# Three more buffers for the second load of q, in the memory of the DFT table, and a new emission order

## The chip, the cores and the metric

The kernel runs on one core of one Trainium2 chip. The time is the device time of one execution in microseconds (us). Five runs of the kernel before gave 229.76, 232.25, 232.29, 233.84 and 233.99 us, with a median of 232.29 us. The core has five engines that run side by side: TensorE (PE) for matmuls, VectorE (DVE) and ScalarE (ACT) for work on elements, GpSimd (POOL), and SyncE (SP), which in this kernel does nothing but issue DMA transfers.

## The reference, cut to what matters

All inputs are bfloat16; S is 2048 positions, D is 640 channels.

```python
g = sigmoid((q * gate_w).sum(-1))
# branch a: a shifted product and a long convolution over positions, by FFT
k_shift = sum over t in 0..3 of k shifted by (3 - t), times shift_k
kv  = k_shift * v
y   = irfft(rfft(kv padded to 2S) * rfft(ssm_k padded to 2S))[:S] + kv * ssm_D
a   = q * y
# branch b: a mixer and an MLP, both with q as the input x
h   = gelu(layernorm(x) @ w1)        # 640 x 640
hs  = (four channel groups of h, shifted by 1, -1, 2, -2 positions) @ w2
x1  = x + hs
b   = x1 + gelu(layernorm(x1) @ w3) @ w4   # 640 x 1536 and 1536 x 640
out = g * a + (1 - g) * b
```

q is needed twice: at the start as x, where it is overwritten step by step by branch b in the tile QX, and at the very end, where y is multiplied by it. That is why it is loaded a second time.

## The kernel before

Positions lie on partitions: partition p holds the 16 consecutive positions 16p to 16p+15. A "slab" s (0 to 15) is the set of 128 positions 16p+s, a 128 x 640 tile. The work is cut into named steps, each made by `pl.add` or `pl.dma` with its dependencies, buffers and function; a step is a handful of instructions on one engine.

Branch b, in chunks of four slabs: `st` and `rs` are the statistics of a layer norm and `xn` the normed slab; it is turned either by TensorE (`tr`, `te`) or by a transposing DMA (`xt`, line 537) into XNT. `W1.c.n` are the matmuls with w1 (line 574), `g1` their gelu on ScalarE; `mx` copies the odd 32-channel pieces on GpSimd. `W2.s` (line 663) makes the second product of a slab, and `add` (line 670) adds it to QX. The second norm leads to `W3.c.f` (line 749), the gelu `g2` (line 753), `W4.s.j` (line 762) and its eviction `w4e` (line 768), which adds it into QX. `xo` (lines 682 and 684) scales QX by 1 - g ahead of that. `m3*` are the steps that make a small DFT matrix on GpSimd, VectorE and ScalarE; the load of w4 (`w4`, line 733) writes over their scratch space and waits for the last of them, `m3n`.

Branch a is a convolution by a DFT in two steps. `k0` to `k3` (`ka`, `kb`, `kc`, `k1`, ...) load k. `km`, `ka` and `kv` (lines 806 to 818) form kv on VectorE, 128 x 1280 at a time; `trh` and `trhe` turn the filter ssm_k. First step: `h1` and `x1` (line 718) multiply the filter and kv by the table F1, `he` and `xe` evict the results, `hw` and `xw` write them to DRAM (GHD, GXD). `tri0` and `tri1` (line 824) make the table of the last step, I1, from F1 by a transposing DMA. Second step, in four rounds: `rh` and `rx` (line 862) load GHD and GXD in another layout into two buffers of RK, `h2`, `x2` and `pv` are matmuls (line 835), `h2e`, `x2e`, `ve` their evictions, `sw` swaps halves between partitions, `pq` (line 895) is the product of the spectra, and `vw` (line 912) writes the result VD to DRAM.

The end, per pair of slabs c: `rv` (line 919) loads 640 KB of VD into one of four buffers VX; `rq` (line 923) loads 320 KB of q into one of two buffers QR, which are the memory of the tile CJ that `km` read before. Per slab s: `iv` (line 931) is the last DFT matmul, `ye` (line 941) its eviction on ScalarE with the factor g, `y` (line 945) the product with q and `ya` (line 951) the sum into QX, both on VectorE; `st` (line 953) stores the slab.

```python
    QR = CJ.rearrange("p (b t) d -> p b t d", b=2)
    r_qr = Ring("qr", 2)
```

The order of the work is written out in the string `ORDER` (lines 85 to 176). Each word is a step, its engine (P, V, A, G, S) and the numbers of its buffers; the words are emitted in that order, so each engine runs its own steps in the order in which they stand there. The waits between engines follow from the dependencies. SyncE has one queue: a DMA that has to wait holds back all that stand behind it. The numbers for cost in `pl.add` and `pl.dma` (`iss`, `rate`, `ndesc`) were used by the planner that made the string; they make no instruction.

Of the kernel before, what the change touches and what calls it, by code (L numbers as in the profile page):

```python
# [10 lines left out]
ALU = mybir.AluOpType  # L11
# [86 lines left out]
mx1.1/G m3i4/G rs0.8/G cj3/G mx1.0/G xn0.9/V/2 xt0.2.1/S/0/2 xn0.8/V/1 st0.15/V xt0.2.0/S/0/1 h1.7.0/P/4/1 he.7.0/A/4/1 hw1/S/2
gt.1/P/2/1 z1/V/2 abs2/A abs3/A rs0.12/G sin3.0/A sin2.0/A m3i0/G h1.6.0/P/6/1 he.6.0/V/6/1 xn0.12/V/0 xt0.3.0/S/1/0 W2.5/P/0
add5/V/0 h1.7.1/P/4/1 he.7.1/A/4/1 h1.6.1/P/2/1 he.6.1/V/2/1 hw3/S/1 rs0.14/G kz/G/0 W2.3/P/6 add3/V/6 km0.0.3/V/0/0 W2.2/P/0  # L100
m3i3/G st1.3/A cj0/A xn0.15/V/2 xt0.3.3/S/1/2 add2/V/0 xn0.14/V/1 W2.4/P/2 h1.12.1/P/6/0 he.12.1/V/6/0 xt0.3.2/S/1/1 add4/V/2
st1.2/A W1.2.3/P/0/0 h1.12.0/P/4/0 g1.2.3/A/0 xn0.13/V/0 xt0.3.1/S/1/0 h1.9.0/P/6/2 W1.2.2/P/1/0 g1.2.2/A/1 he.9.0/V/6/2 cj2/G
W1.2.1/P/2/0 he.12.0/V/4/0 m3i2/G v0/S km0.0.2/V/0/0 h1.13.0/P/6/0 he.13.0/A/6/0 h1.13.1/P/4/0 g1.2.1/A/2 he.13.1/A/4/0 hw6/S/0
h1.9.1/P/0/2 he.9.1/A/0/2 W1.2.4/P/3/0 g1.2.4/A/3 W1.2.0/P/2/0 g1.2.0/A/2 gt.2/P/0/0 st1.4/A m3b/V km0.0.1/V/0/1 h1.11.1/P/6/1
h1.11.0/P/4/1 rs1.2/G xn1.2/V/2 ka0.0.2/V/0/0 xn1.3/V/1 he.11.0/V/4/1 z2/V/0 he.11.1/A/6/1 gt.3/P/1/1 z3/V/1 W1.3.4/P/2/1
h1.10.1/P/6/1 mx2.1/G mx2.0/G m3i5/G km0.0.0/V/0/0 st1.5/A ka0.0.1/V/1/0 gate0/V g1.3.4/A/2 he.10.1/A/6/1 h1.8.1/P/4/2
he.8.1/A/4/2 W1.3.0/P/3/1 g1.3.0/A/3 rs1.4/G h1.14.1/P/0/0 h1.15.1/P/6/0 gate1/A ka0.0.0/V/0/0 kv0/V/0 he.14.1/A/0/0
he.15.1/A/6/0 W1.3.2/P/2/1 g1.3.2/A/2 h1.10.0/P/4/1 W1.3.1/P/3/1 g1.3.1/A/3 h1.14.0/P/0/0 he.14.0/A/0/0 he.10.0/A/4/1
xt1.0.0/S/0/2 xn1.4/V/0 km0.1.3/V/0/0 gate2/V W1.3.3/P/2/1 g1.3.3/A/2 km0.1.2/V/0/1 xn1.5/V/2 ka0.1.2/V/1/0 mx1.2/G
km0.1.1/V/0/0 km0.1.0/V/0/1 xo3/A ka0.1.1/V/0/0 m3i1/G mx2.3/G W2.6/P/6 ka0.1.0/V/1/0 add6/V/6 xt1.0.1/S/0/1 w3/S h1.8.0/P/0/2  # L110
he.8.0/A/0/2 kv2/V/0 W2.7/P/4 add7/V/4 m3c/G m3d/V m3s/A W2.9/P/2 add9/V/2 mx3.2/G xt1.0.2/S/0/0 W2.8/P/0 xt1.0.3/S/0/2
W3.0.7/P/6/0/0 g2.0.7/A/6/0 W3.0.8/P/7/0/1 g2.0.8/A/7/1 xo5/A add8/V/0 h1.15.0/P/4/0 W3.0.3/P/0/0/2 W3.0.4/P/1/0/0
W3.0.9/P/6/0/1 g2.0.4/A/1/0 he.15.0/A/4/0 W3.0.2/P/7/0/2 W3.0.5/P/1/0/0 g2.0.5/A/1/0 g2.0.9/A/6/1 st1.6/A mx3.3/G k1/S/1
km1.0.3/V/1/0 W3.0.11/P/2/0/1 g2.0.11/A/2/1 km1.0.2/V/1/0 st1.7/A km1.0.1/V/1/1 W3.0.1/P/1/0/2 W3.0.6/P/3/0/0 g2.0.1/A/1/2
ka1.0.2/V/0/0 ka1.0.1/V/1/0 km1.0.0/V/1/0 ka1.0.0/V/0/0 v1/S kv4/V/0 km1.1.3/V/1/0 g2.0.2/A/7/2 km1.1.2/V/1/1 ka1.1.2/V/1/0
W3.0.0/P/2/0/2 st1.8/A g2.0.3/A/0/2 xo4/A km1.1.1/V/1/0 ka1.1.1/V/0/0 km1.1.0/V/1/1 ka1.1.0/V/1/0 kv6/V/0 mx2.2/G
W3.0.10/P/1/0/1 g2.0.6/A/3/0 mx3.1/G W2.11/P/4 k2/S/0 hw5/S/1 mx3.0/G W2.13/P/6 m3n/G g2.0.10/A/1/1 w4/S v2/S g2.0.0/A/2/2
W4.3.0/P/0/2/0/1 km2.0.3/V/0/0 km2.0.2/V/0/0 rs1.6/G xn1.7/V/1 xo7/A add11/V/4 w4e3.0/V/0 ka2.0.2/V/0/0 W2.10/P/2 xo2/A
km2.0.1/V/0/1 ka2.0.1/V/1/0 km2.0.0/V/0/0 add13/V/6 k3/S/1 hw4/S/2 xt1.1.1/S/1/1 xn1.6/V/0 add10/V/2 st1.9/A st1.11/A rs1.8/G
W4.2.1/P/0/2/0/1 W4.5.1/P/1/2/0/1 W4.2.0/P/4/2/0/1 xn1.9/V/2 xn1.8/V/1 mx0.3/G xt1.1.0/S/1/0 W4.5.0/P/5/2/0/1 xt1.1.3/S/1/2  # L120
xo6/A ka2.0.0/V/0/0 w4e2.0/V/4 xt1.1.2/S/1/1 kv8/V/0 w4e5.0/V/5 km2.1.3/V/0/0 st1.10/A hw7/S/0 W2.12/P/6 x1.3.1/P/2/1 add12/V/6
w4e5.1/V/1 tri0/S v3/S xe.3.1/A/2/1 tri1/S st1.13/A rs1.10/G st1.12/A rs1.12/G W4.3.1/P/4/2/0/1 W4.4.1/P/1/2/0/1 x1.1.0/P/6/2
xe.1.0/A/6/2 km2.1.2/V/0/1 km2.1.1/V/0/0 ka2.1.2/V/1/0 w4e4.1/V/1 w4e2.1/V/0 x1.3.0/P/2/1 W4.4.0/P/5/2/0/1 xe.3.0/A/2/1
W3.1.10/P/0/1/3 g2.1.10/A/0/3 x1.0.0/P/6/2 xe.0.0/A/6/2 x1.1.1/P/2/2 W3.1.2/P/1/1/0 g2.1.2/A/1/0 xe.1.1/A/2/2 x1.0.1/P/6/2
W3.1.3/P/0/1/0 xe.0.1/A/6/2 xw0/S/2 km2.1.0/V/0/1 ka2.1.1/V/0/0 ka2.1.0/V/1/0 xn1.11/V/0 xt1.2.1/S/0/0 W3.1.8/P/1/1/3
g2.1.8/A/1/3 kv10/V/0 g2.1.3/A/0/0 xn1.10/V/2 W3.1.7/P/2/1/1 g2.1.7/A/2/1 w4e4.0/V/5 km3.0.3/V/1/0 km3.0.2/V/1/0 km3.0.1/V/1/1
w4e3.1/V/4 xt1.2.0/S/0/2 ka3.0.2/V/0/0 x1.2.1/P/6/1 x1.2.0/P/4/1 xe.2.1/V/6/1 xe.2.0/A/4/1 xw1/S/1 x1.6.0/P/0/0 xe.6.0/A/0/0
W3.1.0/P/3/1/0 g2.1.0/A/3/0 ka3.0.1/V/1/0 xn1.12/V/1 x1.6.1/P/6/0 x1.7.1/P/4/0 xe.7.1/A/4/0 xe.6.1/A/6/0 W3.1.5/P/2/1/1
g2.1.5/A/2/1 km3.0.0/V/1/0 x1.8.0/P/0/2 xe.8.0/A/0/2 ka3.0.0/V/0/0 kv12/V/0 x1.7.0/P/4/0 xe.7.0/A/4/0 xt1.2.2/S/0/1 xw3/S/0
xn1.13/V/0 xt1.2.3/S/0/0 W3.1.1/P/3/1/0 x1.9.1/P/6/2 xe.9.1/A/6/2 km3.1.3/V/1/0 km3.1.2/V/1/1 x1.9.0/P/0/2 xe.9.0/A/0/2  # L130
g2.1.1/A/3/0 W3.1.4/P/2/1/1 x1.8.1/P/4/2 xe.8.1/A/4/2 xw4/S/2 x1.13.1/P/6/1 xe.13.1/A/6/1 x1.12.1/P/0/1 W3.1.6/P/3/1/1
km3.1.1/V/1/0 x1.12.0/P/4/1 xe.12.0/A/4/1 g2.1.6/A/3/1 x1.13.0/P/6/1 xe.13.0/A/6/1 xe.12.1/V/0/1 xw6/S/1 ka3.1.2/V/1/0
ka3.1.1/V/0/0 g2.1.4/A/2/1 km3.1.0/V/1/1 ka3.1.0/V/1/0 kv14/V/0 rh0/S/0 rh1/S/1 W3.1.11/P/0/1/3 g2.1.11/A/0/3 W3.1.9/P/1/1/3
x1.11.1/P/4/0 x1.10.0/P/6/0 xe.10.0/A/6/0 xe.11.1/V/4/0 xo11/V W2.14/P/2 g2.1.9/A/1/3 add14/V/2 x1.10.1/P/6/0 xe.10.1/V/6/0
x1.11.0/P/4/0 xe.11.0/A/4/0 xw5/S/0 W3.2.0/P/0/0/2 st1.14/A x1.4.0/P/2/2 xe.4.0/V/2/2 xo8/A xo10/A g2.2.0/A/0/2 x1.5.1/P/4/2
xe.5.1/V/4/2 W2.1/P/6 W2.0/P/2 add1/V/6 xo13/V x1.4.1/P/4/2 st1.1/A x1.5.0/P/0/2 xe.5.0/A/0/2 xo9/V xe.4.1/V/4/2 xw2/S/2
add0/V/2 W2.15/P/6 x1.15.1/P/4/1 xe.15.1/A/4/1 x1.14.1/P/0/1 W3.2.1/P/2/0/2 add15/V/6 st1.0/A xe.14.1/A/0/1 x1.14.0/P/6/1
xe.14.0/V/6/1 x1.15.0/P/4/1 xe.15.0/A/4/1 xw7/S/1 g2.2.1/A/2/2 W3.2.2/P/3/0/2 g2.2.2/A/3/2 rq0/S/0 h2.1.4/P/0/1/0 h2e.1.4/A/0/0
h2.1.3/P/6/1/0 h2e.1.3/V/6/0 h2.0.0/P/4/0/1 W3.2.3/P/2/0/2 h2e.0.0/A/4/1 g2.2.3/A/2/2 h2.0.3/P/0/0/1 h2.1.1/P/6/1/0
h2e.0.3/A/0/1 rs1.0/G xn1.1/V/2 xt1.3.3/S/1/2 W4.8.1/P/3/0/1/3 h2e.1.1/V/6/0 h2.1.2/P/4/1/0 st1.15/A w4e8.1/V/3 h2e.1.2/A/4/0  # L140
# [39 lines left out]
def kernel(  # L180
# [16 lines left out]
    nc = tc.nc  # L197
    P = nc.NUM_PARTITIONS
# [90 lines left out]
    pl = Plan()  # L289
# [9 lines left out]
    r_xin = Ring("xin", 2)  # L299
    r_vx = Ring("vx", 4)  # L300
    r_gy = Ring("gy", 4)
    r_qr = Ring("qr", 2)
    r_xs = Ring("xs", 3)
    r_pq = Ring("pq", 2)
    r_vst = Ring("vst", 2)
# [682 lines left out]
```

## Time and profile before

| what | us |
|---|---|
| the profiled execution's own time | 232.29 |
| its span, from the first to the last instruction | 230.4 |
| around the span | 1.9 |
| TensorE busy | 211.7 |
| VectorE busy | 189.2 |
| ScalarE busy | 165.1 |
| GpSimd busy | 60.0 |
| last W4 groups begin | 199.47 |
| last `iv` matmul ends | 224.55 |
| last VectorE step ends | 227.36 |

In 231 us the DMA engines moved 65.88 MB, a mean of 286 GB/s. A line of a stage reads: its bounds, its length, the busy time and number of instructions of PE, PEld (weight loads), DVE, ACT and POOL, the granted TensorE clock, the mean busy share of the DMA engines, and what they moved in GB/s. A line of waits reads: engine, line, tile, what it waited for, the total in us, how often, and the longest. A line of a timeline reads: start, length, engine, line, operation, tiles, number of instructions; SPq are SyncE's issues of DMAs. The engine's name with a line number such as L945 stands for the source line.

### The profile page before, as it was taken

The numbers are of one execution on the slowest core, as the hardware profiler recorded it, in microseconds if no ns is written. First come the engines' busy times: TensorE is split into PE (matmuls) and PEld (weight loads), VectorE is DVE, ScalarE is ACT, GpSimd is POOL, SyncE is SP. The second block draws the span as 40 slices with busy tenths as digits, with TensorE's granted clock in tenths as the row PEclk, the third lists the DMA queues.
The fourth block names the chain that finished last, engine by engine and source line by source line (L and its number), as shares of the span: only waits on it lengthen the run. The fifth ranks groups of instructions, "written<-read, shape, count | busy, mean of one in ns | idle before, by whom it ended". The sixth has DMA issues, their size and how long they took to land.

```text
span 230.4 us, 4443 instructions
## 1 busy us (share of the span) xinstructions
PE 211.7 (92%) x1626; PEld 123.6 (54%) x1641; DVE 189.2 (82%) x340; ACT 165.1 (72%) x252; POOL 60.0 (26%) x137
## 2 busy tenths in 40 slices
PE   6679999999989799799999999999999999999950
PEld 6557457565634576555566466433355554566630
DVE  8999979979999997999997668998649894076584
ACT  6799989899387554459887951899997884546521
POOL 2645755269997334500001220000000000000000
PEclk9999999999999999999999999999999999999996
DMA  7999979999995995979989979999999963699887
GB/s 211 373 392 294 337 157 255 185 283 335 263 417 135 385 276 81 237 193 244 320 255 378 366 236 344 355 244 350 350 334 335 346 228 133 225 403 344 298 270 268
DMA packets 53029, 65.88 MB, mean 286 GB/s; under 512 B 22544, under 2 KB 39697, under 8 KB 52624
## 3 DMA queue, kind: packets, MB, share of 16 engines
q1 hardware_dynamic: 53008, 65.61, 92.4%
q8 instruction: 12, 0.20, 0.4%
q14 instruction: 9, 0.07, 0.1%
HBM read 37.03 MB, written 18.35 MB: 240 GB/s over the span
## 4 chain that ended last, share of the span: by engine, by line
PE 57%; DVE 13%; DMA 12%; POOL 6%; ACT 6%; issue 3%; SPq 1%; DVEq 0%; POOLq 0%; ACTq 0%
PE PS L762 15%; PE PS L749 14%; PE PS L835 8%; PE PS L718 6%; PE PS L574 5%; PE PS L663 5%; DMA XNT<-XN 3%; DMA RG<-in_A_ssm_k_dram 3%; DMA RK<-GHD 3%; DVE RK L815 3%; DVE RK L811 3%; DMA CJ<-in_A_q_dram 3%; DVE QX L768 2%; DVE RK L945 2%; DVE QX L951 1%
## 5 line engine op out<-in xcount | busy, mean ns | idle before, releaser
L320 ACT CAST SX<-PS 128x640 bf16<-128x640 f32 (+1 forms) x62 | 46.4, 778 | 18.5 <-PE PS L835 10.4
L762 PE MATMUL PS<-W,RG 128*128 128x320 bf16 x384 | 56.2, 299 | 2.8 <-DVE QX L768 1.5
L749 PE MATMUL PS<-XNT,W 128*128 128x512 bf16 x229 | 54.9, 379 | 1.4 <-DVE QX L670 0.8
L762 PEld LDWEIGHTS <-RG 128*128 128x128 bf16 x384 | 36.5, 98 | 22.1 <-issue 8.4
L749 PEld LDWEIGHTS <-W 128*128 128x128 bf16 x240 | 22.6, 98 | 29.1 <-issue 5.5
L753 ACT ACTIVATE RG<-PS 128x512 bf16<-128x512 f32 x48 | 27.9, 607 | 8.5 <-PE PS L749 8.4
L768 DVE SCALAR_TENSOR_TENSOR QX<-PS,ZG,QX 128x320 bf16<-128x320 f32 x32 | 17.1, 546 | 13.7 <-PE PS L762 13.7
L895 DVE TENSOR_TENSOR SX<-SX,R 128x2048 bf16<-128x2048 bf16 x20 | 24.1, 1220 | 4.7 <-ACT SX L320 2.5
L574 PE MATMUL PS<-XNT,R 128*128 128x512 bf16 x96 | 24.0, 379 | 1.2 <-DMA R<-in_B_w_dram 1.0
L718 PE MATMUL PS<-KV,F 128*128 128x320 bf16 x128 | 23.9, 299 | 0.1
L324 DVE CAST SX<-PS 128x640 bf16<-128x640 f32 (+1 forms) x22 | 19.9, 911 | 4.4 <-PE PS L718 2.7
L663 PE MATMUL PS<-R 128*128 128x320 bf16 x160 | 23.4, 299 | 0.0
L941 ACT ACTIVATE RK<-PS,ZG 128x640 bf16<-128x640 f32 x16 | 11.8, 793 | 13.5 <-PE PS L931 10.4
L815 DVE TENSOR_TENSOR RK<-RK 128x1280 bf16<-128x1280 bf16 x24 | 20.6, 860 | 0.4
L811 DVE TENSOR_TENSOR RK<-RK,CJ 128x1280 bf16<-128x1280 bf16 x24 | 20.1, 856 | 0.0
L663 PEld LDWEIGHTS <-R 128*128 128x128 bf16 x160 | 15.7, 98 | 6.4
L320 ACT CAST KV<-PS 128x1024 bf16<-128x1024 f32 x17 | 17.0, 1017 | 2.2 <-PE PS L835 2.2
L718 PEld LDWEIGHTS <-F 128*128 128x128 bf16 x128 | 12.2, 98 | 8.8
L530 DVE TENSOR_SCALAR XN<-QX,MV,RS 128x640 bf16<-128x640 bf16 x32 | 14.5, 464 | 1.5 <-DMA XNT<-XN 1.5
L574 PEld LDWEIGHTS <-R 128*128 128x128 bf16 x100 | 9.5, 98 | 10.3 <-DMA R<-in_B_w_dram 1.2
L523 POOL TENSOR_TENSOR RS<-VE,NHALF 128x2 f32<-128x2 f32 x16 | 13.4, 838 | 1.3
L835 PEld LDWEIGHTS <-M 64*64 64x64 bf16 x320 | 7.6, 105 | 11.4 <-issue 7.0
(104 smaller groups left out, 283.4 us busy)
## 6 DMA issues: line engine op xcount, KB each, us to landing
GHD<-SX SPq DMA_DIRECT2D x8, 640.0 KB, 4.4
GXD<-SX SPq DMA_DIRECT2D x8, 640.0 KB, 4.4
RK<-GHD SPq DMA_DIRECT2D x4, 1280.0 KB, 8.7
RK<-GXD SPq DMA_DIRECT2D x4, 1280.0 KB, 6.6
R<-R SPq DMA_DIRECT2D x8, 640.0 KB, 6.5
VD<-KV SPq DMA_DIRECT2D x4, 1280.0 KB, 6.1
RK<-VD SPq DMA_DIRECT2D x8, 640.0 KB, 5.8
W<-in_B_w_dram SPq DMA_DIRECT2D x2, 1920.0 KB, 8.5
```

Source lines behind the costliest of these rows:

```text
L320: nc.scalar.copy(out=o, in_=i)
L574: nc.tensor.matmul(ps(pb), lhsT=lhsT, rhs=XNT[:, xb.idx, k, :], start=(k == 0), stop=(k == DT - 1))
L663: nc.tensor.matmul(ps(pb)[:, j, 0:DH], lhsT=gst_ap(k, s), rhs=W2[:, k, j * DH:(j + 1) * DH], start=(k == 0), stop=(k == DT - 1))
L718: nc.tensor.matmul(ps(pb)[:, j, 0:DH], lhsT=F1[:, s // 4, h, s % 4, :], rhs=src[:, s, ds], start=True, stop=not dterm)
L749: nc.tensor.matmul(ps(pb), lhsT=W3[:, k, f0 * P:(f0 + 1) * P], rhs=XNT[:, xb.idx, k, :], start=(k == 0), stop=(k == DT - 1))
L753: gns.append(pl.add("g2.%d.%d" % (c, f0), {A: act_p(512)}, lambda e, f0=f0, pb=pb, gb=gb: nc.scalar.activation(out=GTP[:, gb.idx, f0 % 4, ...
L762: nc.tensor.matmul(ps(pb)[:, 0:DH], lhsT=GTP[:, gbs[f // 4].idx, f % 4, i * P:(i + 1) * P], rhs=W4[:, f, j * DH:(j + 1) * DH], start=(f == ...
L768: nc.vector.scalar_tensor_tensor(out=x, in0=ps(pb)[:, 0:DH], scalar=OMG[:, s:s + 1], in1=x, op0=ALU.mult, op1=ALU.add)
L811: m = pl.add("km%d.%d.%d" % (c, u, j), {V: dve(2 * D, .52)}, lambda e, src=src, cj=cj, tb=tb: nc.vector.tensor_tensor(out=TMP[:, tb.idx].r ...
L815: prev = pl.add("ka%d.%d.%d" % (c, u, j), {V: dve(2 * D, .52)}, lambda e, tb=tb: nc.vector.tensor_tensor(out=acc, in0=acc, in1=TMP[:, tb.i ...
L835: nc.tensor.matmul(pt[64 * C:64 * C + 64, R, :], lhsT=M3[64 * R:64 * R + 64, m, :], rhs=rhs_fn(R, C), start=start, stop=stop)
L895: nc.vector.tensor_tensor(out=PQ[:, qb.idx], in0=XS[:, sb.idx].unsqueeze(1).to_broadcast([P, 2, 1024]), in1=HH[:, hhb.idx, u], op=ALU.mult)
```

## The change

The ring of q buffers grows from two to five. The first two remain in CJ; the other three lie in the first 3840 elements of each partition of the table F1. For that, every `rq` now depends, besides the `kv` steps, on all `x1` matmuls, which read F1, and on both `tri` transposes, which read it too. The planner's issue cost of `rh` and `rx` is set to 800 ns. The string ORDER is replaced as a whole; it has the same 942 steps, and 45 of them run on another engine than before (evictions and `xo` between VectorE and ScalarE, two `mx` copies from GpSimd to VectorE). No step is added or removed.

```diff
-    QR = CJ.rearrange("p (b t) d -> p b t d", b=2)
+    CJQ = CJ.rearrange("p (b t) d -> p b t d", b=2)
+    F1Q = F1.rearrange("p g h t d -> p (g h t d)")[:, 0:3840].rearrange("p (b t d) -> p b t d", t=2, d=D)
+
+    def qr(b):
+        return CJQ[:, b.idx] if b.idx < 2 else F1Q[:, b.idx - 2]
...
-    r_qr = Ring("qr", 2)
+    r_qr = Ring("qr", 5)
...
-        qb = Buf(r_qr, kall)
-        lq = pl.dma("rq%d" % c, lambda e, qb=qb, c=c: nc.sync.dma_start(out=QR[:, qb.idx], in_=q3[:, 2 * c:2 * c + 2, :]),
+        qb = Buf(r_qr, kall + xpe + i1n)
+        lq = pl.dma("rq%d" % c, lambda e, qb=qb, c=c: nc.sync.dma_start(out=qr(qb), in_=q3[:, 2 * c:2 * c + 2, :]),
...
-                nc.vector.tensor_tensor(out=GY[:, yb.idx], in0=GY[:, yb.idx], in1=QR[:, qb.idx, s % 2, :], op=ALU.mult)
+                nc.vector.tensor_tensor(out=GY[:, yb.idx], in0=GY[:, yb.idx], in1=qr(qb)[:, s % 2, :], op=ALU.mult)
```

The new order, taken apart by engine at the places that matter (the old one above, the new one below each time):

```text
SyncE, 50 to 90 us
old: xt1.0.0 xt1.0.1 w3 xt1.0.2 xt1.0.3 k1 v1 k2 hw5 w4 v2 k3 hw4 xt1.1.1 xt1.1.0 xt1.1.3 xt1.1.2
new: xt1.0.0 w3 xt1.0.3 xt1.0.1 xt1.0.2 k1 v2 v1 w4 k2 tri1 xt1.1.3 hw4 k3 xt1.1.1 xt1.1.2 xt1.1.0
SyncE, second DFT step
old: rh0 rh1 xw5 xw2 xw7 rq0 xt1.3.3 rx0 sw0.0 sw0.1 rx1 sw1.0 sw1.1 xt1.3.2 xt1.3.1 xt1.3.0 rh2 rq1 vw0
new: rh1 rh0 xw5 xw2 xw7 xt1.3.2 rq0 rx0 sw0.1 sw0.0 sw1.0 rx1 sw1.1 rq2 xt1.3.0 xt1.3.1 xt1.3.3 rh2 rq1 vw0
SyncE, the end
old: vw1 vw2 vw3 rv0 rv1 rv2 rv3 rv4 rq2 rq3 rv7 rv6 rq7 rq4 rv5 st7 st4 rq5 st2 st6 rq6 st5 ...
new: vw1 rq3 vw2 vw3 rq7 rv0 rv1 rv2 rv3 rv4 rv7 rq4 rv5 rv6 rq5 rq6 st7 st6 st1 ...
GpSimd
old: rs1.2 mx2.1 mx2.0 m3i5 rs1.4 mx1.2 m3i1 mx2.3 m3c mx3.2 mx3.3 mx2.2 mx3.1 mx3.0 m3n
new: rs1.2 mx1.2 rs1.4 mx2.3 mx2.2 mx2.0 m3i2 m3i5 m3c mx3.3 m3n mx3.1
TensorE, after the first W3 chunk
old: W2.11 W2.13 W4.3.0 W2.10 W4.2.1 W4.5.1 W4.2.0 W4.5.0 W2.12 x1.3.1 W4.3.1 W4.4.1 ... W3.1.10
new: W2.12 W4.5.1 W4.2.1 W2.10 W4.3.1 W4.4.1 W2.11 W4.5.0 W4.3.0 W3.1.10
TensorE, ahead of the first matmul on rh2
old: pv.1.3 W3.3.8 W3.3.10 x2.1.1 h2.2.3
new: pv.1.3 W3.3.8 W3.3.10 x2.1.4 pv.1.0 x2.1.1 W3.2.10 h2.2.0
TensorE, the end
old: W4.0.0 W4.14.0 iv0 iv1 iv3 iv2 W4.1.1 iv5 iv4 iv6 iv7 W4.1.0 iv8 iv9 W4.14.1 iv15 iv14 W4.15.0 iv12 W4.15.1 iv10 iv11 W4.0.1 iv13
new: W4.14.0 W4.0.0 W4.1.1 iv1 iv0 iv3 iv2 W4.1.0 iv4 iv5 iv7 iv6 W4.15.0 iv9 iv15 iv8 iv14 W4.14.1 iv11 iv10 iv12 iv13 W4.15.1 W4.0.1
VectorE, from the last add of the first norm to the first W4 evictions
new: add8 km1.0.3 km1.0.2 km1.0.1 ka1.0.2 ka1.0.1 km1.0.0 ka1.0.0 kv4 km1.1.3 km1.1.2 km1.1.1 ka1.1.2 xn1.9 ka1.1.1 km1.1.0 ka1.1.0 kv6 km2.0.3 km2.0.2 km2.0.1 xn1.6 xn1.8 xn1.7 ka2.0.2 ka2.0.1 w4e5.1 add10 w4e2.1 w4e3.1 add12 km2.0.0 w4e4.1 add11
```

## The prediction

> **What bounds the kernel now.** I read the page's head first, then the busy time by stage, then the waits of the stages that have any, then SyncE's own issues at the end.
>
> ```profile
> span 230.4 us, 4443 instructions
> PE 211.7 (92%) x1626; PEld 123.6 (54%) x1641; DVE 189.2 (82%) x340; ACT 165.1 (72%) x252; POOL 60.0 (26%) x137
> ```
>
> ```profile
> core 0: us, PE busy (x) PEld busy (x) DVE busy (x) ACT busy (x) POOL busy (x), PEclk, DMA share, GB/s
> 0.00:20.00 20.00, 14.40 (x155) 11.52 (x157) 18.32 (x54) 16.70 (x22) 9.02 (x37) 1.00 0.94 326
> 20.00:60.00 40.00, 39.84 (x321) 24.25 (x323) 36.59 (x86) 36.79 (x64) 24.91 (x52) 1.00 1.00 252
> 60.00:96.00 36.00, 32.30 (x197) 19.23 (x198) 33.82 (x55) 19.07 (x37) 21.35 (x38) 1.00 0.88 267
> 96.00:126.00 30.00, 29.84 (x178) 17.64 (x181) 28.52 (x47) 23.50 (x41) 1.79 (x4) 1.00 0.98 270
> 126.00:158.00 32.00, 31.70 (x271) 15.85 (x271) 25.83 (x32) 23.19 (x33) 2.93 (x8) 1.00 1.03 318
> 158.00:199.40 41.40, 41.22 (x355) 19.82 (x355) 27.36 (x28) 33.43 (x41) 0.00 (x0) 1.00 0.81 280
> 199.40:224.60 25.20, 22.41 (x160) 15.30 (x159) 16.05 (x37) 11.66 (x18) 0.00 (x0) 1.00 0.92 328
> 224.60:230.40 5.80, 0.00 (x0) 0.00 (x0) 2.69 (x6) 0.78 (x1) 0.00 (x0) 0.68 0.75 269
> ```
>
> TensorE is full at full clock from 20 to 199.4 us, except for 3.7 us between 60 and 96. The rest of what it misses is the head (5.6 us) and the end: 2.8 us idle from 199.4 to 224.6, then 5.8 us after its last matmul. A gain has to come from the end or from 60 to 96. These are the waits of the end, what SyncE issues there (L919 loads of VD, L923 loads of q, L953 stores), and the waits of 60 to 96:
>
> ```profile
> DVE RK L945 <- DMA CJ<-in_A_q_dram: 4.9, 3, 2.1
> ...
> PE PS L931 <- DMA RK<-VD: 2.2, 1, 2.2
> ```
>
> ```profile
> 206.20 1.55 SPq L923 DMA_DIRECT2D CJ<-in_A_q_dram  x2
> 207.85 0.89 SPq L919 DMA_DIRECT2D RK<-VD  x2
> 211.91 1.68 SPq L923 DMA_DIRECT2D CJ<-in_A_q_dram  x2
> 213.68 0.39 SPq L919 DMA_DIRECT2D RK<-VD  x1
> ```
>
> ```profile
> PE PS L762 <- DVE QX L768: 1.5, 2, 1.3
> ...
> PE PS L762 <- DMA W<-in_B_w_dram: 1.2, 1, 1.2
> PE PS L749 <- DVE QX L670: 0.8, 1, 0.8
> ```
>
> VectorE waits 4.9 us in three pieces for a load of q. With two buffers, each q load stands in SyncE's queue until a multiply frees a buffer, and the VD loads behind it stand too: the last (rv5) leaves at 213.68, TensorE waits 2.2 us for it, and the last q load (rq6) leaves at 220.84. The chain of waits runs through a q load from 213.24 to 219.44.
>
> **The end, part by part.** *Moved:* three q loads leave the end: rq2 goes to after sw1.1, rq3 between vw1 and vw2, rq7 before rv0. In the end remain rq4, rq5, rq6, each behind a buffer freed long before: SyncE's order is now rv0 to rv4, rv7, rq4, rv5, rv6, rq5, rq6, then the stores. What gates rv5 and rv6 is their slot's last reader, iv5 and iv6.
>
> *TensorE.* Between the start of the last W4 groups (199.47) and the end it has the same 22.4 us of work, so it can't end before 221.8; it ended at 224.55. Twelve W4 matmuls take 1.63 us, an iv (four) 0.54. The new order has three W4 groups ahead of iv1 instead of two: iv1 starts at 199.47 + 3 x 1.63 + 0.2 = 204.5. iv5 then ends near 209.4, iv6 near 210.5 (one W4 between), so rv5 leaves at about 209.5 instead of 213.7 and rq6 at about 211.5 instead of 220.8. At the 5.8 us of a VD load and 5.0 of a q load everything has landed by about 217. iv11 wants rv5 at 216: no wait.
>
> *VectorE.* Before, it ran from y0 (204.30) to ya13 (227.36): 23.1 us, with 2.16 + 12.87 + 2.69 = 17.7 busy and 5.4 idle, of which 4.9 were q. Now y0 waits for ye0, which comes second on ScalarE: 204.5 + 1.58 (first iv to first y in the trace) + 0.69 (one ye) = 206.8. From the 17.7 drop out w4e10.1, w4e1.1 (0.5 each) and xo15 (0.4), which now lie earlier: 16.3 us remain, so 223.1 if nothing is late; I add 0.6 for the pieces of waiting that weren't q, 223.7. From the last VectorE instruction to the end of the span the trace has 3.04 us (a store): 226.7.
>
> *DMA.* From 199.4 to the end 9.82 MB moved (the rates of that stretch times their times). Three q loads of 0.328 MB less is 8.84 MB; at the 366 GB/s seen from 199.4 to 204 that is 24.2 us, to 223.6. VectorE and the DMA engines are thus late together, and stores bunch: I add 0.5 us. The end comes at 227.2, 3.2 us earlier.
>
> **What the moved loads push.** One rule speaks against it: the Trainium skill, page "DMA: Bandwidth & Descriptors", section "Queues, rings and completion order", says each DMA engine takes descriptors in ring order, so a load issued early goes ahead of all that is issued after it. For rq7 the rule makes rv0 0.9 us later (0.328 MB at 366 GB/s). The rows say nothing: SyncE waits 4.6 us there for VD's last write to land while the 190 to 199 us stretch has the engines half idle, so rq7's bytes go in that hole; I take 0. rq3 falls where the share is 0.81: 0. For rq2 the rule is serious: 126 to 158 us has share 1.03 at 318 GB/s, and behind rq2 stand three transposes and rh2, whose landing (150.77, 6.7 us) released TensorE directly. By the rule rh2 lands 1.0 us later, plus 0.35 to 0.57 us for issuing it. But in the new order pv.1.0 and W3.2.10 (0.43 + 1.08) come before the first matmul on rh2, 1.5 us of cover. I take 0; uncovered it costs 1.5. Reordering rh0/rh1 and sw0/sw1 moves loads by one issue each (0.4 us): 0. The iss=800 only feeds the planner's books, no instruction.
>
> **60 to 96 us.** *Gained:* GpSimd's m3n, for which the load of the W4 weights waits, now stands behind one mx copy instead of five (63.71 to 68.65 in the trace, about 1 us each), so that load leaves SyncE some 4 us before 70.7 and the 1.2 us wait goes. The 0.8 us (add8) probably goes too, since the first W3 groups now use banks that add7 and add9 free. *Risked:* k1 now has two transposes ahead of it that wait for VectorE (xn1.3, xn1.4), before one (xn1.5); by one transpose (1.2 to 2.8 us) it leaves later than 57.76. VectorE's km1.0.3 started at 64.80 with k1 there; it could now start between 63.9 and 66. From it to w4e5.1, the first W4 eviction, stand 21 of the 128x1280 operations and four xn: 16 took 14.8 us in the trace (64.80 to 79.6), five more take 4.0, the xn 1.6: w4e5.1 at 84.8 to 86.9. TensorE, with W2.12, W4.5.1, W4.2.1, W2.10 and W4.3.1 (2 x 1.36 + 3 x 1.63 = 7.6) from 75.7, is at 83.3 when W4.4.1 needs w4e5.1's bank: it waits 1.5 to 3.6 us, where before it waited 0.8 + 1.2 + 1.5 = 3.5 in this stage. The stage stands at -2.0 to +0.6 (the upper end with 0.5 more for W3.1.10's bank). VectorE, 33.8 busy of 36, also hands ScalarE two evictions and two xo more than it takes over between 60 and 126 us, a help of some 2 us. Against it, the transposes for W3.1 wait for xn1.6 to xn1.8, now together at 83 to 85, and take 3.8 us each to land, close to W3.1.10 at 94. I take the stage at 0.
>
> The other rearrangements (head, 20 to 60, 158 to 199) exchange neighbours on engines that stay full; nothing there can gain over 0.5 us, each can lose a bubble: bounds -0.5 to +2, taken 0 as the old order's 0.7 us in these stages is the nearest row.
>
> **Sum.** Against its own execution: 230.4 - 3.2 = 227.2 of span; around it lie 232.29 - 230.4 = 1.9 us: 229.1. That execution is also the median of the five.
>
> **Rivals.** *Slower: the VectorE chain between 64 and 90.* w4e5.1 ends 20.9 us after km1.0.3 starts (20.4 and its own 0.5), and km1.0.3 can't start before k1 has landed. From k1 at 69.1 on, w4e5.1 ends after 90.0 and TensorE's wait at W4.4.1 passes 6.7 us: the old 3.5 plus the 3.2 won at the end; beyond that each us is a us of the kernel. At 71 it is 8.6 us, 1.9 too much: 234.2. For it: VectorE is busy 94% there, loads of k take 7.8 us in the median, and a transpose takes up to 4.2 us to issue when the queue is full. Against: k1 must come 5 us later than it did by one or two transposes. Chance 0.17.
>
> *The end is paced by the DMA engines.* If they keep the stretch's own mean, 9.82 MB in 31.0 us or 317 GB/s, 8.84 MB last to 227.3; the last 3 us ran at half rate (164 GB/s), so the last store is done some 1.5 us after: 228.8, and 230.7 in all. For: the share is 0.98 to 1.03 from 199.4 to 206.5. Against: 0.89 at 308 GB/s from 206.5 to 224.6, where SyncE held loads back. Chance 0.18.
>
> *Both stages gain.* The old waits go and the new bank wait is short (-2.0): 227.1. Chance 0.17.
>
> **Numbers.** My case, 229.1, has 0.48 and by itself spans 227.9 to 230.5. Two per cent is 4.6 us, about what a measurement of this kernel can tell from no change (its runs lie from 229.8 to 234.0). Faster by that (below 227.6): most of the third rival and the edge of mine, 0.2. Slower (above 236.9): the far end of the slow rival, 0.07. The range to hold 8 in 10 reaches from inside the third rival to the slow one: 226.4 to 234.4.
>
> **What would show it.** Right: no VectorE wait on q loads over 0.5 us after 199; rq6 issued by 213; VectorE without holes from y0 to the end; a span near 227. Wrong in the end: TensorE waits on VD loads, or the store queue ends more than 4 us after VectorE. Wrong in the middle: TensorE idle above 4 us between 75 and 96, released by L768. Wrong about rq2: a TensorE hole before the first h2.2 matmul. If the start of the last W4 groups is more than 1.5 us away from 199.5, the middle decided the result, not the buffers.

## The result and the profile after

The changed kernel takes 229.45 us (median of 25 runs, 228.08 to 230.74). The kernel before, on the same chip, takes 232.06 us (46 runs). The ratio is 0.9908, with a 95% interval of 0.9889 to 0.9928. Here and below a ratio is taken from the fast runs alone (some executions, of every kernel, are a few us slower) and against runs of the kernel before from the same batch, so it isn't the quotient of the two medians. The prediction was 229.1 (226.4 to 234.4). The gain is real, but smaller than the 2% that the forecast counted as faster.

The profiled execution of the changed kernel took 229.26 us. Its span is 227.3 us, against 230.4 before. Line numbers are four higher than before: the loads of VD are L923, those of q L927, the `iv` matmuls L935, the multiply by q L949, ScalarE's eviction of an `iv` L945, the sum into QX L955, W2 L667 with its add L674, W4 L766 with its eviction L772, W3 L753, the second step's matmuls L839, its loads L866 and its swaps L882. In the kernels of the experiments all of these are two lower.

The head of the page after:

```profile
span 227.3 us, 4442 instructions
PE 212.9 (94%) x1624; PEld 125.3 (55%) x1641; DVE 190.8 (84%) x343; ACT 164.2 (72%) x251; POOL 64.1 (28%) x135
```

The stages after, with the bounds of the table before except the last. The columns are length, busy time of PE, PEld, DVE, ACT and POOL, granted clock, DMA share, GB/s:

```profile
60.00:96.00 36.00, 34.03 (x205) 20.02 (x206) 35.56 (x59) 21.68 (x40) 19.38 (x28) 1.00 1.09 290
96.00:126.00 30.00, 29.79 (x180) 17.75 (x182) 25.64 (x42) 24.20 (x43) 5.62 (x11) 1.00 0.83 269
126.00:158.00 32.00, 31.89 (x283) 15.97 (x284) 27.96 (x36) 24.43 (x33) 1.72 (x5) 1.00 1.03 309
158.00:199.40 41.40, 39.52 (x340) 19.43 (x336) 27.39 (x28) 31.12 (x39) 0.00 (x0) 1.00 0.83 290
199.40:224.60 25.20, 22.14 (x160) 15.26 (x157) 17.89 (x40) 12.38 (x17) 0.00 (x0) 1.00 0.94 334
224.60:227.30 2.70, 0.00 (x0) 0.00 (x0) 0.00 (x0) 0.00 (x0) 0.00 (x0) 0.77 0.51 179
```

Two of these rows stand out, in opposite directions. TensorE gained 1.7 us of work from 60 to 96 (34.03 against 32.30) and lost 1.7 us from 158 to 199.4 (39.52 against 41.22). So the end still begins when it did: the last run of W3 matmuls starts at 191.59, before at 191.65. (The first 20 us, not shown, have 1.3 us more TensorE time as well, but the long first W3 run, which now has five matmuls more, begins only 0.5 us earlier, at 64.46 against 64.93.) The last matmul now ends at 221.84, before at 224.55; behind it the kernel needs 5.5 us, before 5.8.

What SyncE issues from 198 us on:

```profile
198.55 8.67 SPq L923 DMA_DIRECT2D RK<-VD  x6
207.68 0.35 SPq L927 DMA_DIRECT2D CJ<-in_A_q_dram  x1
209.58 1.45 SPq L923 DMA_DIRECT2D RK<-VD  x2
211.08 0.46 SPq L927 DMA_DIRECT2D F<-in_A_q_dram  x1
212.65 0.34 SPq L927 DMA_DIRECT2D CJ<-in_A_q_dram  x1
214.44 10.59 SPq L957 DMA_DIRECT2D out_dram<-QX  x16
```

The last VD loads (rv5, rv6) leave at 209.58, before at 213.68. The last q load (rq6) leaves at 212.65, before at 220.84. The waits of the same stretch, where before VectorE waited 4.9 us for q and TensorE 2.2 us for VD:

```profile
DVE QX L772 <- PE PS L766: 11.1, 2, 8.5
...
DVE RK L949 <- ACT RK L945: 1.0, 1, 1.0
```

There is no wait for q and no TensorE wait for VD left. The two waits shown are over by y0 (206.75), and from there VectorE runs without a hole to its end at 223.51.

TensorE's waits of over 0.5 us from 60 to 199 us (start, length, instructions, and in brackets the wait before them):

```profile
61.20 1.52 PE L667 MATMUL PS<-R 128*128 128x320 bf16 x10 [0.62 <-DVE QX L674]
64.46 12.03 PE L753 MATMUL PS<-XNT,W 128*128 128x512 bf16 x54 [0.60 <-DVE QX L674]
84.69 1.79 PE L766 MATMUL PS<-W,RG 128*128 128x320 bf16 x12 [0.59 <-DVE QX L772]
165.59 0.63 PE L839 MATMUL PS<-RK,M 64*64 64x512 bf16 x8 [1.21 <-DMA RK<-GHD]
184.20 1.79 PE L766 MATMUL PS<-W,RG 128*128 128x320 bf16 x12 [0.52 <-DVE QX L772]
```

The first three sum to 1.8 us; before, that stage had 3.5 us. The last two are new: 1.7 us in a stage that had none of that size.

### The profile page after: what moved, and what is told of

Read it like the earlier page. It is cut to its first block, busy times and chain, and to the rows that moved or that the text cites. A ratio compares the mean times of both kernels' runs of the same rounds, so it can differ in the third digit from the quotient of the medians.

```text
span 227.3 us, 4442 instructions
## 1 busy us (share of the span) xinstructions
PE 212.9 (94%) x1624; PEld 125.3 (55%) x1641; DVE 190.8 (84%) x343; ACT 164.2 (72%) x251; POOL 64.1 (28%) x135
## 4 chain that ended last, share of the span: by engine, by line
PE 58%; DVE 17%; DMA 15%; issue 4%; SPq 2%; ACT 2%; DVEq 0%; ACTq 0%
PE PS L753 20%; PE PS L766 16%; PE PS L839 6%; PE PS L722 5%; DMA RG<-in_A_ssm_k_dram 5%; PE PS L667 5%; DMA RK<-GHD 4%; DMA R<-R 4%; PE PS L578 4%; DVE RK L949 3%; DVE QX L955 2%; DVE RK L815 2%; DVE RK L819 2%; DVE QX L772 2%; DMA GHD<-SX 2%
## 5 line engine op out<-in xcount | busy, mean ns | idle before, releaser
L324 ACT CAST SX<-PS 128x640 bf16<-128x640 f32 (+1 forms) x64 | 47.4, 770 | 14.8 <-PE PS L722 7.0
L766 PE MATMUL PS<-W,RG 128*128 128x320 bf16 x384 | 56.2, 299 | 1.4 <-DVE QX L772 1.1
L753 PE MATMUL PS<-XNT,W 128*128 128x512 bf16 x228 | 55.5, 379 | 1.2 <-DVE QX L674 0.6
L766 PEld LDWEIGHTS <-RG 128*128 128x128 bf16 x384 | 36.6, 98 | 20.7 <-issue 6.2
L753 PEld LDWEIGHTS <-W 128*128 128x128 bf16 x240 | 22.6, 98 | 28.6 <-issue 5.3
L772 DVE SCALAR_TENSOR_TENSOR QX<-PS,ZG,QX 128x320 bf16<-128x320 f32 x32 | 17.2, 546 | 13.0 <-PE PS L766 13.0
L667 PE MATMUL PS<-R 128*128 128x320 bf16 x160 | 23.8, 299 | 0.6 <-DVE QX L674 0.6
L328 DVE CAST SX<-PS 128x640 bf16<-128x640 f32 (+1 forms) x20 | 18.4, 919 | 3.9 <-PE PS L839 1.8
L815 DVE TENSOR_TENSOR RK<-RK,CJ 128x1280 bf16<-128x1280 bf16 x24 | 20.6, 879 | 0.0
L819 DVE TENSOR_TENSOR RK<-RK 128x1280 bf16<-128x1280 bf16 x24 | 19.9, 828 | 0.4
L667 PEld LDWEIGHTS <-R 128*128 128x128 bf16 x160 | 15.7, 98 | 7.2 <-issue 0.8
L945 ACT ACTIVATE RK<-PS,ZG 128x640 bf16<-128x640 f32 x16 | 11.8, 792 | 8.5 <-DVE QX L772 5.3
L324 ACT CAST KV<-PS 128x1024 bf16<-128x1024 f32 x16 | 15.7, 1019 | 0.7 <-PE PS L839 0.7
L674 DVE SCALAR_TENSOR_TENSOR QX<-PS,QX 128x640 bf16<-128x640 f32 x16 | 12.9, 816 | 3.2 <-PE PS L667 3.2
L507 ACT ACTIVATE RG<-QX 128x640 bf16<-128x640 bf16 x16 | 11.8, 740 | 5.0 <-DVE QX L674 4.9
L578 PEld LDWEIGHTS <-R 128*128 128x128 bf16 x100 | 9.6, 98 | 10.2 <-DMA R<-in_B_w_dram 1.2
L330 DVE TENSOR_SCALAR R<-PS 128x1024 bf16<-128x1024 f32 x9 | 10.7, 1220 | 4.6 <-PE PS L839 4.6
```

Source lines behind the costliest of these rows:

```text
L324: nc.scalar.copy(out=o, in_=i)
L328: nc.vector.tensor_copy(out=o, in_=i)
L578: nc.tensor.matmul(ps(pb), lhsT=lhsT, rhs=XNT[:, xb.idx, k, :], start=(k == 0), stop=(k == DT - 1))
L667: nc.tensor.matmul(ps(pb)[:, j, 0:DH], lhsT=gst_ap(k, s), rhs=W2[:, k, j * DH:(j + 1) * DH], start=(k == 0), stop=(k == DT - 1))
L753: nc.tensor.matmul(ps(pb), lhsT=W3[:, k, f0 * P:(f0 + 1) * P], rhs=XNT[:, xb.idx, k, :], start=(k == 0), stop=(k == DT - 1))
L766: nc.tensor.matmul(ps(pb)[:, 0:DH], lhsT=GTP[:, gbs[f // 4].idx, f % 4, i * P:(i + 1) * P], rhs=W4[:, f, j * DH:(j + 1) * DH], start=(f == ...
```

## The experiments

To compare the ends of kernels that arrive there at different times, I measure from the start of the last run of W3 matmuls to the end of the span, called "the end" below. It is 38.75 us before (230.4 - 191.65) and 35.7 us after (227.3 - 191.59), so all of the 3.1 us of span is won in it. This matters because in some profiled executions the granted clock of the first 20 us is below 1.00 and everything after starts later.

### The end: buffers or order

The diff has two parts. The first try to do each alone missed its aim, and tells something else than its expectation. The number of the q buffer also stands in the words of the `y` steps, and the last word wins. I had moved only the `rq` words.

**Early loads into two buffers (e1_buffers_alone).** Old order, q loads moved early:

```diff
-... sw1.1 xt1.3.2 ... vw1 vw2 vw3 rv0 rv1 rv2 rv3 rv4 rq2/S/0 rq3/S/1 rv7 rv6 rq7/S/0 rq4/S/1 rv5 st7 st4 rq5/S/0 st2 st6 rq6/S/1
+... sw1.1 rq2/S/2 xt1.3.2 ... vw1 rq3/S/3 vw2 vw3 rq7/S/4 rv0 rv1 rv2 rv3 rv4 rv7 rv6 rq4/S/1 rv5 rq5/S/0 rq6/S/2
```

> The old emission order, with five q buffers; only the q loads are moved: rq2 to behind sw1.1, rq3 to behind vw1, rq7 to behind vw3, rq5 and rq6 to directly behind rv5. Theory A (the buffers win at the end, the new order wins nothing overall): 229.0 to 230.5 us, no wait of VectorE for q after 199 us, the last W4 groups begin within 1 us of 199.5. Theory B (the gain is the new order's, the buffers alone do nothing since the VD loads follow as before): 231.5 to 232.5 us.

In fact the kernel still used two buffers. By the order of its steps, rq2 and rq7 overwrite the buffer of rq0 before y0 reads it, so nine slabs were multiplied with rows of q that belong to others, and rq4 had to wait for a buffer. It took 234.5 us, ratio 1.0101 (1.0047 to 1.0154). It says nothing about the buffers.

**Five buffers, late loads (e2_order_alone).** New order, with the q loads back at the places they have in the old queue:

```diff
-... sw1.1 rq2 xt1.3.0 ... vw1 rq3 vw2 vw3 rq7 rv0 rv1 rv2 rv3 rv4 rv7 rq4 rv5 rv6 rq5 rq6
+... sw1.1 xt1.3.0 ... vw1 vw2 vw3 rv0 rv1 rv2 rv3 rv4 rq2 rq3 rv7 rv6 rq7 rq4 rv5 rq5 rq6
```

> The new emission order with two q buffers: rq2 and rq3 stand behind rv4, rq7 and rq4 behind rv6, rq5 and rq6 behind rv5, each waiting for its buffer as in the old kernel. Theory A: 231.3 to 232.8 us, VectorE waits 3 to 5 us for q after 199 us. Theory B: 229.2 to 230.2 us. In both, the start of the last W4 groups stays within 0.7 us of the 199.2 of the changed kernel, or comes up to 1 us earlier if the early load of rq2 cost something.

Here the `y` words kept all five buffers. So this is the changed kernel with its q loads late: 231.5 us, ratio 0.9974 (0.9935 to 1.0013), end 38.6 us. Its waits at the end:

```profile
PE PS L933 <- DMA RK<-VD: 3.0, 2, 2.4
DVE RK L947 <- DMA CJ<-in_A_q_dram: 2.7, 2, 2.4
```

Free buffers alone don't win. The two waits that the change removed are both back. They aren't all due to the q loads: this queue also has rv6 ahead of rv5, as the old one has, while the new order needs rv5 first, and rv5 left at 212.26, in the changed kernel at 209.58. And the wait has a second cost, which the granted clock shows:

```profile
219.56 3.94 PE L933 MATMUL PS<-RK,I 128*128 128x320 bf16 x16 [2.36 <-DMA RK<-VD]
```

These 16 matmuls take 2.34 us in the changed kernel. Here they take 1.6 us more, since the granted clock from 219.4 to 222.7 was 0.51. How the end splits between the q loads, rv5 and the clock was not tried.

**Buffers alone (e1b_buffers_alone).** The same places as in e1, with the buffer numbers of the `y` steps set to match:

```diff
-y5/V/0/0 y4/V/2/0 y7/V/3/1 y6/V/1/1 y15/V/3/0 y14/V/0/0 y12/V/0/1 y13/V/3/1
+y5/V/0/2 y4/V/2/2 y7/V/3/3 y6/V/1/3 y15/V/3/4 y14/V/0/4 y12/V/0/2 y13/V/3/2
```

> The old emission order on all engines, with five q buffers and the q loads early (rq2 behind sw1.1, rq3 behind vw1, rq7 ahead of rv0, rq5 and rq6 behind rv5), and now with the buffer numbers of the y steps set to match. Theory A (the buffers win at the end): VectorE's 4.9 us of waiting for q and TensorE's 2.2 us for VD are gone, rq6 is issued by 213; the old order still has VectorE's extra 1.4 us of evictions at the end and, with no cover in front of h2.2, a hole of 0.5 to 1.5 us before it: 229.5 to 231, ratio 0.99 to 0.995. Theory B (the new order wins): no more than 0.5 us, 231.5 to 232.5, ratio 0.997 or above.

It took 232.32 us (12 runs), ratio 1.0008 (0.9962 to 1.0053): no gain. Its profiled execution shows two opposite terms. The end is 36.8 us, 1.9 shorter than before. The waits there:

```profile
ACT RK L943 <- PE PS L933: 9.0, 7, 3.8
DVE RK L947 <- ACT RK L943: 3.4, 4, 2.1
```

VectorE no longer waits for q. But it waits 3.4 us, before 0.3, for ScalarE's eviction of an `iv`, and ScalarE waits for TensorE, which itself waits only 0.6 us for VD. In the old order TensorE doesn't deliver the `iv` fast enough to use the q that is there. The other term lies in the second step:

```profile
156.94 0.41 PE L837 MATMUL PS<-RK,M 64*64 64x512 bf16 x4
158.59 0.63 PE L837 MATMUL PS<-RK,M 64*64 64x512 bf16 x8 [1.23 <-DMA RK<-GHD]
```

Up to 150.7 TensorE is where it was before (150.68 against 150.70). The hole of 1.23 us is then the whole delay of the last W3 run (192.87 against 191.65). The load rh2 left at 151.85, before at 150.77, because rq2 takes 1.17 us to issue ahead of it. The sum, +1.2 - 1.9, is a profile 0.7 us shorter (229.7 against 230.4), which the interval of the ratio can't tell from nothing. The time is what theory B expected here.

**Order alone (e2b_order_alone).** New order, two buffers, the q loads as late as in the old queue, and the `y` words set to the two buffers:

```diff
-    r_qr = Ring("qr", 5)
+    r_qr = Ring("qr", 2)
...
-... vw1 rq3 vw2 vw3 rq7 rv0 rv1 rv2 rv3 rv4 rv7 rq4 rv5 rv6 rq5 rq6
+... vw1 vw2 vw3 rv0 rv1 rv2 rv3 rv4 rq2 rq3 rv7 rv6 rq7 rq4 rv5 rq5 rq6
```

> The new emission order with two q buffers and the q loads where the old kernel has them. Theory A: VectorE waits 4 to 6 us for q at the end as in the kernel before, TensorE 2 to 3 us for VD; no gain: 231.5 to 233, ratio 0.998 to 1.005. Theory B: most of the gain is here too, 229.5 to 230.5, ratio 0.99.

It took 237.54 us, ratio 1.0236 (1.0175 to 1.0296): slower than the kernel before by more than either theory had. The end is 43.1 us. Its waits there:

```profile
DVE RK L947 <- DMA CJ<-in_A_q_dram: 7.2, 4, 3.5
ACT RK L943 <- DVE QX L770: 5.3, 1, 5.3
ACT RK L943 <- DVE QX L953: 4.7, 2, 3.4
PE PS L933 <- DMA RK<-VD: 4.3, 2, 2.8
```

The new order asks for q and VD earlier than the two-buffer queue can bring them. VectorE's wait for q grows from 4.9 to 7.2 us and TensorE's for VD from 2.2 to 4.3. Two things of this kernel aren't the order's: rv6 again stands ahead of rv5, which left at 216.39, and the clock fell again. After a wait of 2.79 us for VD the next 16 `iv` matmuls took 4.00 us in place of 2.34, and the granted clock from 222.3 to 225.7 was 0.52. After the wait of 2.2 us in the kernel before it stayed at 1.00.

The ends of five kernels side by side, in us from the start of the last W3 run:

| | q loads late | q loads early |
|---|---|---|
| old order, two buffers | 38.75 (before) | - |
| old order, five buffers | - | 36.8 |
| new order, two buffers | 43.1 | - |
| new order, five buffers | 38.6 | 35.7 (after) |

Each is one profiled execution. "Order" here takes in the steps that moved to another engine. In the old order the buffers with their early loads are worth 1.9 us, in the new order 7.4. The order is worth -4.4 with two buffers and +1.1 with five. Up to 1.7 us of the 43.1 and of the 38.6 are the lower clock; without it the buffers would still be worth more in the new order (some 5.7 us) than in the old. Theory A, that the buffers win and the order is an accompaniment, and theory B, that the order wins, both fall: neither part gains anything measurable alone.

### The second DFT step

**rq2 moved (e3_rq2_late).** Is rq2, the load that the prediction worried about, the cause of the hole at 165.59?

```diff
-... rx1 sw1.1 rq2 xt1.3.0 ... vw3 rq7 rv0
+... rx1 sw1.1 xt1.3.0 ... vw3 rq7 rq2 rv0
```

> The changed kernel with rq2 moved from behind sw1.1 to behind rq7. Theory C (the 0.33 MB in the crowded stretch makes the loads of the second DFT step later; TensorE's hole of 1.2 us before h2.3 and VectorE's waits for the swaps come from it): the hole shrinks to under 0.4 us, 228.3 to 228.9 us. Theory D (the hole comes from the order of vw0 and rh3 in the queue and from the step itself, not from rq2): hole still 0.9 to 1.5 us, 229.2 to 229.8 us.

It took 229.98 us, ratio 0.9878 (0.9826 to 0.9930), not to be told from the changed kernel's 0.9908. The hole before h2.3 shrank from 1.21 to 0.42 us, but another of 1.85 us stood before matmuls on GXD at 172.58. The time fits neither theory. Its first 20 us ran at a clock of 0.91, and TensorE came to h2.3 at 165.78, in the changed kernel at 164.38, so the smaller hole doesn't say what rq2 does. The five-buffer kernel with late loads says more: it has rq2 late too, its head ran at 1.00, and TensorE came at 164.49. The hole there is 0.86 us, and rh3 landed at 165.3 (156.51 and 8.8), 0.2 us earlier than in the changed kernel.

**Three q loads moved (e6_three_q_late).**

```diff
-... xt1.3.2 rq0 rx0 ... sw1.1 rq2 xt1.3.0 xt1.3.1 xt1.3.3 rh2 rq1 vw0 ... vw1 rq3
+... xt1.3.2 rx0 ... sw1.1 xt1.3.0 xt1.3.1 xt1.3.3 rh2 vw0 ... vw1 rq0 rq2 rq1 rq3
```

> The changed kernel with rq0, rq2 and rq1 all moved to directly behind vw1, so that 0.98 MB leave the stretch from 126 to 158 us and go where the DMA engines are at 0.6 of their time. Theory C: hole before h2.3 gone, swaps land 1 to 2 us sooner, 227.4 to 228.4 us. Theory D: 229.0 to 229.8 us. Slower (above 230) would mean that the loads now get in the way of the writes of VD.

It took 229.14 us, ratio 0.9848 (0.9798 to 0.9897), span 226.8 us. The hole before h2.3 is gone. A smaller one of 0.56 us stands before matmuls on GXD at 169.44, and the one before W4 at 184.12 is 0.83 us. The last W3 run begins at 191.51, as in the changed kernel (191.59). So the hole is as theory C has it, but the time is in theory D's range and not to be told from the changed kernel's, and the swaps did not land sooner (a median of 8.7 us, in the changed kernel 8.6).

**rh3 earlier (e8_rh3_earlier).** The read that frees rh3's buffer is moved ahead of one W3 group:

```diff
-... pv.1.3 W3.3.8 W3.3.10 x2.1.4 pv.1.0 x2.1.1 W3.2.10 h2.2.0
+... pv.1.3 W3.3.8 x2.1.4 x2.1.1 W3.3.10 pv.1.0 W3.2.10 h2.2.0
```

> The changed kernel with x2.1.4 and x2.1.1 moved ahead of W3.3.10, so that the last read of rh3's buffer ends 1.17 us earlier. Theory G (the hole of 1.21 us before h2.3 is rh3's own chain: buffer free, issue, 9.2 us to land): rh3 is issued near 155.2, the hole falls below 0.3 us, and the last W4 groups start up to 1.2 us earlier if nothing else takes the place. Theory H (the second step is paced further down, by the swaps and the products on VectorE): the hole goes or shrinks, but another of the same size opens before the x2.3 or pv.3 matmuls, and the time stays at 229.2 to 229.7.

It took 229.57 us, ratio 0.9903 (0.9873 to 0.9934). That is the time which theory H had, though no hole of the old size opened further down. The load rh3 left 1.0 us earlier, as planned. SyncE's timeline has its issue:

```profile
155.33 0.36 SPq L864 DMA_DIRECT2D RK<-GHD  x1
```

The view of the line of these loads, for the stretch around that issue, has its time to landing:

```profile
DMA to landing us min/median/max: 10.2/10.2/10.2
```

In the changed kernel the chain that ended last holds the same load and, further down, a swap:

```profile
156.35 9.20 DMA RK<-GHD
...
173.19 9.14 DMA R<-R
```

155.33 + 10.2 and 156.35 + 9.20 are the same moment, 165.5. Leaving earlier didn't bring the data earlier. The hole before h2.3 is gone here only because TensorE came to it later: three smaller waits of 0.2 to 0.3 us stand ahead of it and behind it, and between its first W3 run and its last it needs 126.7 us (65.12 to 191.86), the changed kernel 127.1. In the three-load experiment the same view reads:

```profile
DMA to landing us min/median/max: 7.8/7.8/7.8
```

There the load left at 156.49 and landed at 164.3. So taking the three q loads out of the queue ahead did bring it, by 1.2 us; rq2 by itself brought 0.2. How much of this is their bytes, and how much the time that issuing them takes (rh2 left 0.9 us earlier too), is not separated. From 156 to 166 the DMA engines' share is 1.06. It is the rule which the prediction weighed and set aside: the Trainium skill, page "DMA: Bandwidth & Descriptors", section "Queues, rings and completion order", has each DMA engine consume descriptors in ring order. That bytes queued ahead delay a load agrees with it here; that an earlier issue brings nothing in a full queue is what the rh3 experiment shows.

### Starting the `iv` earlier

**e5_iv_earlier.** The third W4 group ahead of the first `iv` is moved behind three of them, on a free bank:

```diff
-W4.14.0 W4.0.0 W4.1.1/P/2 iv1 iv0 iv3 iv2 W4.1.0
+W4.14.0 W4.0.0 iv1 iv0 iv3 iv2 W4.1.1/P/5 W4.1.0
```

> The changed kernel with the third W4 group (W4.1.1) moved behind the first three iv, on a free bank, so that iv1 starts 1.63 us earlier (202.9 in place of 204.5) and y0 near 205. Theory E (VectorE's chain from y0 paces the end): VectorE ends 0.8 to 1.6 us earlier, span -0.8 to -1.5, ratio to the kernel before 0.985 to 0.988. Theory F (the DMA engines pace the end: 8.84 MB from 199.4 on at 366 GB/s last to 223.6 whatever VectorE does, and rv0 lands only near 203.3): the span moves by less than 0.4 us, ratio as the changed kernel's 0.99.

It took 230.03 us, ratio 0.9929 (0.9896 to 0.9963): no gain over the changed kernel. Its profiled execution had the lowest clock in the head of all:

```profile
0.00:20.00 20.00, 14.33 (x142) 12.99 (x144) 16.28 (x48) 13.78 (x19) 7.91 (x34) 0.83 0.93 325
```

So I read it from its own last W3 run (195.09). The first `iv` and y0 come 1.63 us earlier than in the changed kernel, as planned. But VectorE ends at 32.05 us, where the changed kernel ends at 31.92. Its timeline shows where the lead went:

```profile
212.22 1.00 DVE L770 SCALAR_TENSOR_TENSOR QX<-PS,ZG,QX 128x320 bf16<-128x320 f32 x2
214.45 0.49 DVE L947 TENSOR_TENSOR RK<-RK,CJ 128x640 bf16<-128x640 bf16 x1 [1.22 <-ACT RK L943]
```

VectorE now does one more W4 eviction after y0 (0.5 us) and waits 1.22 us for an `iv` that stands behind two W4 groups. Theory E falls. Theory F isn't shown by this either, since VectorE was not made to end earlier. The end was 35.4 us, 0.3 shorter, inside the 0.4 of theory F.

Not tried: the old order with five buffers and rq2 behind the second step, which would say whether the hole is all that keeps the buffers from gaining alone; and a few of VectorE's last sums on GpSimd, which is idle there, which would tell whether VectorE or the DMA engines hold the end now.

## Why the prediction was right, and where it wasn't

**The end, step by step.** The sum held, and nearly every term of it.

| step | predicted | measured |
|---|---|---|
| first `iv` | 204.5 | 204.50 |
| rv5 leaves | 209.5 | 209.58 |
| rq6 leaves | 211.5, by 213 | 212.65 |
| y0 | 206.8 | 206.75 |
| VectorE ends | 223.7 | 223.51 |
| from there to the end of the span | 3.5 (3.04 + 0.5) | 3.8 |
| end of span | 227.2 | 227.3 |

The bytes were right too: 25.2 us at 334 GB/s and 2.7 at 179 make 8.9 MB, predicted 8.84. What the sum did not say is that its two halves depend on each other. It put the 3.2 us down to the loads that leave early and counted the lighter VectorE list beside it. The runs show that the loads alone shorten the end by 1.9 us, and that the same order with two buffers and late loads lengthens it by 4.4, up to 1.7 of it by the lower clock.

**60 to 96 us, taken at 0 of -2.0 to +0.6.** It gained 1.7. The load of W4's weights left at 65.29, 5.4 us before the old 70.71, and its wait is gone, as predicted. The term that was mis-sized is TensorE's wait at W4.4.1: 1.5 to 3.6 predicted, 0.59 measured. w4e5.1 came a little earlier than the forecast (it ended at 84.6, predicted 84.8 to 86.9), and TensorE came later: its first W3 run took 12.03 us from 64.46, so it reached W4.4.1 at 84.1, not at 83.3. W3.1.10 did not wait at all.

**158 to 199 us, taken at 0 of -0.5 to +2.** It lost 1.7, inside the bounds but not at 0. What missed it is the line that these rearrangements "exchange neighbours on engines that stay full". It looks at the engines alone. The prediction's own stage row has the DMA engines full as well, at a share of 1.03 from 126 to 158 (the 0.81 of the row behind it is a mean, with 1.02 from 156 to 166), and TensorE's lead from 60 to 96 ran into that. Here are the issue of rh3 and the first matmuls on it, before:

```profile
158.19 0.36 SPq L862 DMA_DIRECT2D RK<-GHD  x1
166.22 0.60 PE L835 MATMUL PS<-RK,M 64*64 64x512 bf16 x8
```

After, rh3 leaves at 156.35 and TensorE comes to its first use at 164.38. Both are 1.84 us earlier, so the time between them, which has to hide the load, is 8.03 us in both kernels. But the load took 7.8 us before and takes 9.2 now: it landed at 166.0 and lands at 165.55. Before, it was in time by 0.2 us; now it is 1.2 us late. The order of the matmuls isn't the reason. The order-alone kernel has the same order on TensorE here, its first 20 us ran at a clock of 0.91, and TensorE came to h2.3 as late as in the kernel before:

```profile
158.30 0.36 SPq L864 DMA_DIRECT2D RK<-GHD  x1
166.26 0.63 PE L837 MATMUL PS<-RK,M 64*64 64x512 bf16 x8
```

There rh3 took 7.9 us and TensorE did not wait. The swaps of the third round show the same as rh3: they left 3.8 us earlier than before (162.3 against 166.1), and the later of the two landed at 172.9, before at 173.1. With the rh3 experiment this says that in this stretch the DMA engines set the time of arrival, and an earlier TensorE waits for them.

The cover that the prediction named, pv.1.0 and W3.2.10 ahead of the first matmul on rh2, did work: there is no hole before h2.2, and with the early rq2 and no cover, in the buffers-alone kernel, there is one of 1.23 us (priced at 1.5).

The second of the two waits, 0.52 us at 184.20, stands behind a product on VectorE that waits for swaps. Those of the fourth round landed at 182.3, before at 181.3. The median over all swaps is 8.6 us against 6.5, and 8.7 with the three q loads out of the stage, so these loads aren't the reason; it stays open. After this wait TensorE is where it was before (184.20 against 184.24).

So the middle came out at 0 as +1.7 and -1.7, and these are not two independent errors: most of the lead was lost because the loads came no earlier. The prediction had 0 for each as a point within a range, without this link. That its total agrees is in this part luck.

**rq2, rq7, rq3, taken at 0.** For rq7 and rq3 nothing was seen against it. For rq2 the answer depends on the order: hidden in the new one at h2.2, 1.2 us in the old one. Of the 1.2 us by which rh3 lands earlier with all three q loads away, some 0.2 are its own.

**The rivals.** The slower VectorE chain did not come: k1 left at 58.83 (57.76 before) and km1.0.3 started at 65.21, inside 63.9 to 66. An end paced by the DMA engines, at 230.7, did not come either, but their share of 0.94 there is near full. After the change TensorE ends at 221.84, VectorE at 223.51 and the last store about 3.8 us on, so three resources are late together. "Both stages gain" was right for 60 to 96; the 1.7 us were lost again 75 us later, at loads that came no earlier. Faster by over 2% was given 0.2, and did not happen; within 2% had 0.73.

## What to carry to other kernels

A lead won on one engine is worth what the next full resource lets through: here 1.8 us of TensorE's met loads that landed almost when they had before. Read the DMA share of a stage beside its busiest engine. An early load and an order that can use it are one change; test them apart before crediting either, since here each alone gained nothing measurable and the order alone, with its loads queued as before, cost 2.4%. Where the DMA engines are full, ask which bytes stand ahead of a load, not when it is issued.

## What the runs showed of the hardware

- A 1280 KB load that left 1.0 us earlier into a full queue (share 1.06) took 1.0 us longer and landed at the same moment, 165.5. With three q loads out of the stage it took 7.8 us in place of 9.2.
- A 320 KB load issued right behind swaps and ahead of transposes held SyncE's queue for 0.69 to 1.47 us in five kernels (1.15 in the changed one), while at the end of the changed kernel such an issue takes 0.34 to 0.46.
- The granted clock of the first 20 us was 1.00, 0.91 or 0.83 in the profiled executions of kernels that share most of this head. At 0.91, in the buffers-alone kernel, TensorE had caught up by 150 us, since the waits from 60 to 96 took up the delay. At 0.83, in the kernel with the earlier `iv`, the last W3 run still began 3.5 us late.
- After TensorE had waited 2.36 and 2.79 us for a load near the end, its granted clock was 0.51 and 0.52 for the next 3.3 and 3.4 us, and 16 matmuls took 3.94 and 4.00 us in place of 2.34. After a wait of 2.22 us in the kernel before it stayed at 1.00.
